# A state-space scan and a long convolution on one core: every fourth time is scanned, three states per block of four are rebuilt, and the whole order is written anew

## Chip, cores and metric

The kernel runs on 1 core of a Trainium2 chip. The metric is device time in microseconds, the median of a few executions. Before the change it is 246.62 us (3 runs, 243.36 to 247.5). A difference is told as a share of the time before.

## What is computed

Two independent halves share one output of 2048 times by 1280 columns, in bfloat16. In the left half a diagonal complex recurrence with 640 states reads x (2048 x 640):

```
Lam_bar = exp(dt * Lam);  Bu = x @ B_bar.T          (complex, 640 states)
h_t = Lam_bar * h_(t-1) + Bu_t                      (t = 0 .. 2047)
y_t = 2 * Re(C h_t) + x_t * Dskip
```

The right half takes q, k, v (2048 x 640 each): k is shifted and weighted with four taps per column, multiplied by v, convolved per column with a kernel of length 2048 (ssm_k, plus a skip ssm_D), and multiplied by q.

## The kernel before

Everything stands in one program of some 500 named steps (`make_plan`), each with an engine and a function. A string, `ORDER`, lists the steps in the order in which they are issued; a step `name@slot` takes that PSUM slot. There are four PSUM tiles of two banks. Each engine runs its own steps in that order and waits on the others by semaphores, so a step that waits holds up all that stands behind it on its engine or DMA queue.

Left half. The 640 states are five blocks j of 128, on the partitions; time lies along the free dimension. x is loaded transposed on SyncE's queue (`load_x`, L372). Time is cut in two chunks c of 1024 and each chunk into odd and even times, so there are four loads of 512 x 640: x01, x00 for the first chunk, x11, x10 for the second. B is loaded (B0 on SyncE, the rest, B1, on ScalarE's queue), transposed by matmuls against an identity (bt) and evicted (bte). For each block n = 5c + j:
- zo: ten matmuls with the odd x (five per real and imaginary part), evicted by ScalarE (zoe) into zo with one column of history.
- z: ten matmuls with the even x and four with diagonal matrices of Lam_bar (diagL, L404 to L408) that fold in the odd input just before, evicted to z (ze).
- rs (`dve_scan`, L424): VectorE turns z by a table of cosines and sines (L419 to L422), which makes the recurrence real, and scans real and imaginary part with the decay rr2 (L430).
- rout (`dve_out`, L433): VectorE turns back; the result is the state at even times.
- od (`dve_odd`, L439): VectorE makes the state at odd times from it, in five instructions (L443 to L447).

The second chunk starts from a carry (L449). Then p (`pe_proj`, L455) multiplies 128 times of either parity by C, with x times a diagonal of Dskip added; ScalarE evicts to one of two yo tiles (L477) and GpSimd stores it (yd, L481).

Right half, for five blocks G of 128 columns: k and v come transposed (kT, vT, SyncE); kS, a copy of k with its halves of partitions swapped (GpSimd's queue); four taps as matmuls with diagonal weights (dS, tap); VectorE multiplies by v from PSUM (kv, L532); the product goes to memory (kvo, L535) and comes back as rows (kvs, L505). The convolution is a Fourier transform in two matmul stages for kv (s1k, s2k) and for the kernel's rows (hs, s1h, s2h), each evicted by ScalarE; VectorE multiplies the spectra (y, L566 to L574, two halves); two inverse stages follow, with a DMA transpose between them (inv, zs, zt, fin); VectorE multiplies by q from PSUM (ob, L608; q's load is qi, L598), in the tile from which GpSimd stores the result (od_, L613).

A DMA is issued by its engine in order, too: SyncE's queue carries all transposing loads and hs, GpSimd's carries kS, kvo, kvs, qi, od_ and yd.

Of the kernel before, what the change touches and what calls it, by code (L numbers as in the profile page):

```python
# [9 lines left out]
ALU = mybir.AluOpType  # L10
# [32 lines left out]
class Kernel:  # L43


    def __init__(self, ctx, tc, out, ins):
# [19 lines left out]
        for n in ("lre", "lim", "dtf", "theta", "rho", "rr", "rr2", "fr", "kf", "sin1", "aph1", "cos1", "nr", "ni", "den",  # L66
                  "t0", "rden", "ra"):
            t(n, [128, NT], f32)
        t("dt_b", [128, NT])
        t("Fi", [128, NT], i32)  # L70
        t("cmul", [128, NT], i32)
        t("phc", [128, NT], i32)
        t("gam", [128, 3, NT], f32)
        t("lam", [128, 3, NT], f32)
        t("lamb", [128, 3, NT])
        t("rots", [128, NT, 2], f32)
        t("rotc", [128, NT, 2], f32)
# [12 lines left out]
        t("dcol_b", [128, 32 * NG])  # L90
# [36 lines left out]
        self.aph = self.zz[:, 7168:8192].bitcast(f32)  # L127
        self.gph = flat(self.Hf).bitcast(i32).rearrange("p (q a b) -> p q a b", q=4, a=4)
# [21 lines left out]
    def load_B(self, eng, lo, hi):  # L150
        for r, ap in enumerate((self.A_B_re, self.A_B_im)):
            eng.dma_start(out=self.Bn[:, r, lo:hi, :], in_=ap.rearrange("(j i) d -> i j d", i=128)[:, lo:hi, :])

    def load_sk(self):
        src = self.B_shift_k.rearrange("(g h d) s -> h d g s", h=2, d=64)
        for v in range(2):
            for h in range(2):
                self.nc.gpsimd.dma_start(out=self.sk_b[64 * h:64 * h + 64, :, v, :], in_=src[h ^ v])

    def pool_consts(self):  # L160
# [3 lines left out]
        g.iota(self.lo, pattern=[[2, CW]], base=0, channel_multiplier=0)  # L164
        g.iota(self.c30[:], pattern=[[0, 1]], base=2 ** 30, channel_multiplier=0)

    def pool_consts2(self):
        g = self.nc.gpsimd
        g.iota(self.c26[:], pattern=[[0, 1]], base=2 ** 26, channel_multiplier=0)
        g.iota(self.cmul[:], pattern=[[0, NT]], base=2 * CW, channel_multiplier=0)  # L170
        g.iota(self.ccol[:], pattern=[[1, 4]], base=0, channel_multiplier=0)
        g.iota(self.r_ph[:].rearrange("p (k r) -> p k r", r=2), pattern=[[4, 16], [0, 2]], base=1, channel_multiplier=0)
        g.iota(self.r_q16[:].rearrange("p (k r) -> p k r", r=2), pattern=[[0, 16], [16, 2]], base=0, channel_multiplier=0)
# [98 lines left out]
    def dve_gamma(self):  # L272
# [3 lines left out]
        ni = self.lam[:, 1, :]  # L276
        v.tensor_scalar_add(out=nr, in0=self.lam[:, 0, :], scalar1=-1.0)
# [29 lines left out]

    def pool_rot(self):
        self.nc.gpsimd.tensor_tensor(out=self.phc[:], in0=self.cmul[:], in1=self.Fi[:], op=ALU.mult)

    def act_rot(self):
        a = self.nc.scalar.activation
        a(out=self.rots[:, :, 0], in_=self.phc[:], func=ACT.Sin, scale=-SC)
        a(out=self.rots[:, :, 1], in_=self.phc[:], func=ACT.Sin, scale=SC)
        a(out=self.ra[:], in_=self.phc[:], func=ACT.Abs, scale=SC)
        for r in range(2):
            a(out=self.rotc[:, :, r], in_=self.ra[:], func=ACT.Sin, bias=self.hpi[:, 0:1], scale=-1.0)
# [54 lines left out]
    def load_x(self, c, p):  # L372
        self.nc.sync.dma_start_transpose(
            out=self.__dict__[f"xT{c}{p}"][:],
            in_=self.x2[2 * CW * c:2 * CW * c + 2 * CW, :].rearrange("(m p) (k d) -> p m k d", p=2, d=128)[p])

    def pe_z(self, n, p, r, ps, last=True):
        c, j = divmod(n, NT)
        xT = self.__dict__[f"xT{c}{p}"]
        for k in range(NT):  # L380
# [506 lines left out]
```

## Time and profile before

| | before |
|---|---|
| median of 3 runs | 246.62 us |
| the profiled execution: its time, its span | 247.58, 245.7 us |
| TensorE busy (pipelined, modelled ends) | 197.2 us, 80% |
| VectorE busy | 180.7 us, 74% |
| ScalarE busy | 152.0 us, 62% |
| GpSimd busy | 64.8 us, 26% |
| DMA, share of 16 engines: SyncE's, GpSimd's, ScalarE's queue | 52.6%, 26.3%, 2.3% |
| granted TensorE clock, mean | 0.961 |

The span is the time from the first to the last instruction of one profiled execution. A busy share is a mean over stages with different limits, so the table alone doesn't tell what the time hangs on: for that one looks at stretches of the span, at what an engine waited for, and at the chain of work that ended last. PE is TensorE, DVE VectorE, ACT ScalarE, POOL GpSimd, SP SyncE; a q behind a name is that engine's DMA queue.

### The profile page before, as it was taken

The numbers are of one execution on the slowest core, as the hardware profiler recorded it, in microseconds if no ns is written. First come the engines' busy times: TensorE is split into PE (matmuls) and PEld (weight loads), VectorE is DVE, ScalarE is ACT, GpSimd is POOL, SyncE is SP. The second block draws the span as 40 slices with busy tenths as digits, with TensorE's granted clock in tenths as the row PEclk, the third lists the DMA queues.
The fourth block names the chain that finished last, engine by engine and source line by source line (L and its number), as shares of the span: only waits on it lengthen the run. The fifth ranks groups of instructions, "written<-read, shape, count | busy, mean of one in ns | idle before, by whom it ended". The sixth has DMA issues, their size and how long they took to land.

```text
span 245.7 us, 5441 instructions
## 1 busy us (share of the span) xinstructions
PE 197.2 (80%) x2295; PEld 140.8 (57%) x2306; DVE 180.7 (74%) x303; ACT 152.0 (62%) x187; POOL 64.8 (26%) x91
## 2 busy tenths in 40 slices
PE   0266996977796699989629999989758999985991
PEld 0162342435444678767426579776756598764770
DVE  2749399999999999999606973897559999950030
ACT  2648395976976657645325888896638999442121
POOL 8897692025000220015051120010501100110231
PEclk9999799999999799999958999999989999999998
DMA  3999999999920689498969989409993503829634
GB/s 57 248 180 24 190 237 224 193 191 228 172 56 2 183 166 111 89 168 240 102 134 196 241 176 221 75 0 124 218 196 72 119 21 65 128 55 185 149 117 121
DMA packets 80698, 34.87 MB, mean 142 GB/s; under 512 B 76001, under 2 KB 77281, under 8 KB 80673
## 3 DMA queue, kind: packets, MB, share of 16 engines
q1 hardware_dynamic: 73936, 18.75, 52.6%
q0 software_dynamic: 4368, 14.46, 26.3%
q10 hardware_dynamic: 2368, 1.31, 2.3%
q8 instruction: 18, 0.29, 0.5%
q14 instruction: 8, 0.06, 0.1%
HBM read 9.52 MB, written 7.86 MB: 71 GB/s over the span
## 4 chain that ended last, share of the span: by engine, by line
DVE 15%; issue 13%; PE 12%; DMA 12%; POOL 2%; ACT 1%; DVEq 1%; POOLq 0%; ACTq 0%
DMA out_dram<-yo 5%; DMA zz<-zz 4%; DMA qb<-in_B_q_dram 3%; PE ps L465 2%; DVE rot L571 2%; DVE Xs L572 2%; PE ps L381 2%; DVE Xs L574 2%; PE ps L527 2%; DVE z L430 2%; DVE vT L532 1%; POOL out_dram L613 1%; DVE rot L419 1%; DVE rot L420 1%; DVE qb L608 1%
## 5 line engine op out<-in xcount | busy, mean ns | idle before, releaser
L381 PE MATMUL ps<-xT,BT 128*128 128x512 bf16 x189 | 48.3, 387 | 6.0 <-ACT zz L144 2.1
L465 PE MATMUL ps<-Cs,h 128*128 128x320 bf16 x320 | 48.3, 299 | 0.0
L381 PEld LDWEIGHTS <-BT 128*128 128x128 bf16 x200 | 19.1, 99 | 28.7 <-issue 5.9
L465 PEld LDWEIGHTS <-h 128*128 128x128 bf16 x320 | 29.3, 98 | 10.2
L477 ACT CAST yo<-ps 128x640 bf16<-128x640 f32 x16 | 11.0, 692 | 38.9 <-PE ps L469 25.7
L608 DVE TENSOR_TENSOR qb<-ps,qb 128x1024 bf16<-128x1024 f32 x10 | 12.1, 1219 | 26.0 <-PE ps L603 16.0
L558 PE MATMUL ps<-As_kv,Gre 128*128 128x128 bf16 x80 | 18.5, 231 | 8.8 <-ACT yo L477 6.6
L564 ACT CAST Xs<-ps 128x1024 bf16<-128x1024 f32 x20 | 19.2, 1028 | 7.2 <-PE ps L561 6.4
L559 PEld LDWEIGHTS <-nGim 128*128 128x128 bf16 x160 | 16.5, 103 | 12.4 <-issue 10.7
L564 ACT CAST Hf<-ps 128x1024 bf16<-128x1024 f32 x20 | 19.5, 1046 | 6.4 <-PE ps L561 5.3
L548 ACT CAST As_h<-ps 128x1024 bf16<-128x1024 f32 x20 | 20.1, 1041 | 5.3 <-PE ps L544 5.3
L590 ACT CAST zz<-ps 128x1024 bf16<-128x1024 f32 x20 | 19.5, 1026 | 3.3 <-PE ps L585 2.5
L548 ACT CAST As_kv<-ps 128x1024 bf16<-128x1024 f32 x20 | 19.5, 1030 | 1.5 <-PE ps L544 1.5
L559 PE MATMUL ps<-As_h,nGim 128*128 128x128 bf16 x80 | 18.3, 229 | 1.3 <-DVE nGim L343 1.3
L532 DVE TENSOR_TENSOR vT<-ps,vT 128x1024 bf16<-128x1024 f32 x10 | 11.9, 1213 | 10.1 <-PE ps L527 10.1
L558 PE MATMUL ps<-As_h,Gre 128*128 128x128 bf16 x80 | 18.3, 229 | 1.3 <-DVE qb L608 1.0
L582 PE MATMUL ps<-Xs,Hre 128*128 128x128 bf16 x80 | 17.6, 219 | 1.4 <-DVE Xs L574 1.4
L561 PE MATMUL ps<-As_kv,Gre 128*128 128x128 bf16 x80 | 18.5, 232 | 0.0
L560 PE MATMUL ps<-As_kv,Gim 128*128 128x128 bf16 x80 | 18.5, 232 | 0.0
L559 PE MATMUL ps<-As_kv,nGim 128*128 128x128 bf16 x80 | 18.5, 232 | 0.0
L560 PE MATMUL ps<-As_h,Gim 128*128 128x128 bf16 x80 | 18.3, 228 | 0.0
L561 PE MATMUL ps<-As_h,Gre 128*128 128x128 bf16 x80 | 18.3, 228 | 0.0
(166 smaller groups left out, 528.8 us busy)
## 6 DMA issues: line engine op xcount, KB each, us to landing
h_st<-in_B_ssm_k_dram SPq DMA_DIRECT2D x10, 256.0 KB, 5.7
qb<-in_B_q_dram POOLq DMA_DIRECT2D x5, 512.0 KB, 6.8
kv_rows<-vT POOLq DMA_DIRECT2D x5, 512.0 KB, 4.7
kv_st<-kv_rows POOLq DMA_DIRECT2D x10, 256.0 KB, 7.1
out_dram<-yo POOLq DMA_DIRECT2D x8, 320.0 KB, 3.4
out_dram<-qb POOLq DMA_DIRECT2D x5, 512.0 KB, 6.8
kS<-kT POOLq DMA_DIRECT2D x10, 129.0 KB, 4.7
zz<-in_A_B_re_dram ACTq DMA_DIRECT2D x1, 640.0 KB, 7.6
```

What stands on the lines that cost most here:

```text
L381: self.nc.tensor.matmul(ps, lhsT=self.BT[:, r, k, j * 128:(j + 1) * 128], rhs=xT[:, k, :], start=(k == 0), stop=(last and k == NT - 1))
L465: mm(o[:, 0:320], lhsT=h[:, p, r, ts], rhs=self.Cs[:, r, j, c0:c0 + 320], start=(j == 0 and r == 0), stop=False)
L532: self.nc.vector.tensor_tensor(out=self.vT[:, ts], in0=ps[:].rearrange("p a n -> p (a n)"), in1=self.vT[:, ts], op=ALU.mult)
L548: self.nc.scalar.copy(out=As[:].rearrange("p k (h s) -> p h k s", h=2)[:, :, :, 16 * q:16 * q + 16], in_=ps[:].rearrange("p h (k s) -> p h ...
L558: mm(o_re, lhsT=self.Gre[:, k1, :], rhs=re, start=True, stop=False)
L559: mm(o_re, lhsT=self.nGim[:, k1, :], rhs=im, start=False, stop=True)
L560: mm(o_im, lhsT=self.Gim[:, k1, :], rhs=re, start=True, stop=False)
L561: mm(o_im, lhsT=self.Gre[:, k1, :], rhs=im, start=False, stop=True)
L564: self.nc.scalar.copy(out=dst[:, :, o:o + 128 * n], in_=ps[:] if n == 4 else ps.rearrange("p (r n) -> p r n", r=2))
L582: mm(o_re, lhsT=self.Hre[:, k1, :], rhs=yre, start=True, stop=False)
L590: self.nc.scalar.copy(out=self.Zs[:, :, 2 * ks[0]:2 * ks[0] + n, :].rearrange("p i k c -> p k i c"), in_=psf.rearrange("p (k i c) -> p k i ...
L608: self.nc.vector.tensor_tensor(out=self.qb[:, :, cs].rearrange("p a (i c) -> p a i c", c=4), in0=ps[:].rearrange("p a n -> p (a n)").rearr ...
```

## The change

- Left half: time is no longer cut into chunks. It is split by its remainder p to 4, so there are four loads of 512 x 640 (x0 to x3, every fourth time), and tiles F{p}{j} hold the input sums and later, in place, the states. Per block j the inputs are summed in the order 1, 2, 3, 0: z1 takes ten matmuls, z2, z3 and z0 take ten and four with diagL that add Lam_bar times the sum before. For z2 of blocks 0 to 2 that addition is made by VectorE instead (zd2, `dve_odd` with q = 1). One scan per block, over 512 columns with the decay rr4, needs z0, and so all four x. The rotation back gives the state at p = 0 in place (h0); three `dve_odd` rebuild the states at p = 1, 2, 3 (h1, h2, h3) with the powers Lam, Lam^2, Lam^3, which a new step `pow` makes. Chunk, carry, history and their steps are gone.
- The projection takes 128 groups of four times; a store holds two of the four remainders.
- B comes block by block: eight loads of 160 KB, all on SyncE's queue, behind x1. lre moves from ScalarE's to GpSimd's queue.
- The shift taps come by one load, and their swapped half by two copies from SBUF to SBUF that wait for it. The skip column ssm_D comes in runs of 61 elements instead of single ones.
- The order of all steps is new.

```
     def load_x(self, p):
         self.nc.sync.dma_start_transpose(out=self.__dict__[f"xT{p}"][:],
                                          in_=self.x2.rearrange("(m p) (k d) -> p m k d", p=NP, d=128)[p])
...
+        prev = None if p == 1 or (p, j) in BYDVE else (self.F(p - 1, j) if p else self.__dict__[f"F3{j}"][:, :, 1:1 + CW])
+        for r in range(2):
+            for k in range(NT):
+                mm(ps[:, r, :], lhsT=self.BT[:, r, k, j * 128:(j + 1) * 128], rhs=xT[:, k, :], start=(k == 0),
+                   stop=(prev is None and k == NT - 1))
+            if prev is not None:
+                mm(ps[:, r, :], lhsT=self.diagL[:, 0, j, :], rhs=prev[:, r, :], start=False, stop=False)
+                mm(ps[:, r, :], lhsT=self.diagL[:, 2 - r, j, :], rhs=prev[:, 1 - r, :], start=False, stop=True)
...
+    def dve_odd(self, p, j, q=0):
+        v = self.nc.vector
+        h, s = self.F(q, j), self.F(p, j)
+        l = [self.lam[:, p - q - 1, i, j:j + 1] for i in range(3)]
+        v.tensor_scalar_mul(out=self.rot_p, in0=h, scalar1=l[0])
+        v.tensor_scalar_mul(out=self.rot_x[:, 0, :], in0=h[:, 1, :], scalar1=l[2])
+        v.tensor_scalar_mul(out=self.rot_x[:, 1, :], in0=h[:, 0, :], scalar1=l[1])
+        v.tensor_tensor(out=s, in0=s, in1=self.rot_p, op=ALU.add)
+        v.tensor_tensor(out=s, in0=s, in1=self.rot_x, op=ALU.add)
...
     def load_sk(self):
-        src = self.B_shift_k.rearrange("(g h d) s -> h d g s", h=2, d=64)
-        for v in range(2):
-            for h in range(2):
-                self.nc.gpsimd.dma_start(out=self.sk_b[64 * h:64 * h + 64, :, v, :], in_=src[h ^ v])
+        g = self.nc.gpsimd
+        g.dma_start(out=self.sk_b[:, :, 0, :], in_=self.B_shift_k.rearrange("(g d) s -> d g s", d=128))
+        for h in range(2):
+            g.dma_start(out=self.sk_b[64 * h:64 * h + 64, :, 1, :], in_=self.sk_b[64 - 64 * h:128 - 64 * h, :, 0, :])
...
+            src = bass.AP(src.tensor, src.offset, [[1, 4], [128, NG], [1, 61]])
+            g.dma_start(out=self.dcol_b[64 * h:64 * h + 64:16, :, 0:61], in_=src)
...
-pc l_lim l_ldt B0 l_lre B1 x01 pc2 dc zer gp1 exp dc2 bt0@0 dt bt1@2 pp rho bte0@0 rr x00 G1 gp0 Fi aRM bte1@2 bt6@0 l_sk bt5@4
+pc l_ldt B0 x1 l_dsk dc l_lre exp l_lim gp2 bt1@0 bt0@2 B1 bte1@0 gp0 bte0@2 B2 B3 gp1 zer z10@2 B4 dt pc2 rho x2 Fi rr G2 tp0
```

On SyncE's queue at the start of the program, behind the first load of B and of x (xT are the loads of x, Cs those of C, h_st the rows of the kernel), there stands before:

```order
L373 DMA_TRANSPOSE xT_142<-in_A_x_dram 128x5x512
L494 DMA_TRANSPOSE kT<-in_B_k_dram 128x2048
L505 DMA h_st<-in_B_ssm_k_dram 64x16x128 x2
L494 DMA_TRANSPOSE vT<-in_B_v_dram 128x2048
L680 DMA_TRANSPOSE Cs<-in_A_C_re_dram 128x5x640
L680 DMA_TRANSPOSE Cs<-in_A_C_im_dram 128x5x640
L373 DMA_TRANSPOSE xT_145<-in_A_x_dram 128x5x512
L373 DMA_TRANSPOSE xT_144<-in_A_x_dram 128x5x512
```

and now, behind x1 and the other eight loads of B:

```order
L361 DMA_TRANSPOSE xT_141<-in_A_x_dram 128x5x512
L445 DMA_TRANSPOSE kT<-in_B_k_dram 128x2048
L445 DMA_TRANSPOSE vT<-in_B_v_dram 128x2048
L629 DMA_TRANSPOSE Cs<-in_A_C_re_dram 128x5x640
L361 DMA_TRANSPOSE xT_147<-in_A_x_dram 128x5x512
L629 DMA_TRANSPOSE Cs<-in_A_C_im_dram 128x5x640
L361 DMA_TRANSPOSE xT_129<-in_A_x_dram 128x5x512
L456 DMA h_st<-in_B_ssm_k_dram 64x16x128 x2
```

The rows h_st have moved behind the last x. The last x (x0, xT_129), which the first scan needs now, has the same transposing loads ahead of it as the last of before (xT_144).

On VectorE, around the first scan of the program (z_154 is block 0's z), there stands before:

```order
L515 TENSOR_TENSOR diagS<-id_70,sk_b 128x512
L291 TENSOR_TENSOR diagD<-ident,dsk_raw 128x640
L419 TENSOR_TENSOR rot<-tabs,z_154 128x1024
L420 TENSOR_TENSOR rot<-tabs,z_154 128x1024
L422 TENSOR_TENSOR rot<-rot 128x512 x2
L430 SCALAR_TENSOR_TENSOR z_154<-rr_84,rot 128x512 x2
```

and now (F_132 is F02, the sum of block 2 at p = 0):

```order
L466 TENSOR_TENSOR diagS<-id_70,sk_b 128x512
L331 TENSOR_SCALAR nGim<-Gim 128x2048
L302 SCALAR_TENSOR_TENSOR Cs<-Cs,gam,As_kv 128x640
L304 SCALAR_TENSOR_TENSOR Cs<-Cs,gam,As_kv 128x640
L382 TENSOR_TENSOR rot<-tabs,F_132 128x1024
L383 TENSOR_TENSOR rot<-tabs,F_132 128x1024
L385 TENSOR_TENSOR rot<-rot 128x512 x2
L392 SCALAR_TENSOR_TENSOR F_132<-rr_84,rot 128x512 x2
```

The diagS here is block 1's; the first block's stands ahead of diagL. The first scan has moved behind both kv products of block 0, three of five blocks of C and nGim.

On GpSimd's queue, in the middle of the program (vT to kv_rows is kvo, kv_rows to kv_st is kvs, out from qb is od_, qb from q is qi, out from yo is yd), there stands before:

```order
L535 DMA kv_rows<-vT 128x2048
L481 DMA out_dram<-yo_148 256x1x640
L613 DMA out_dram<-qb 128x16x128
L501 DMA kS<-kT 64x2x516 x2
L481 DMA out_dram<-yo_147 256x1x640
L598 DMA qb<-in_B_q_dram 128x16x128
L505 DMA kv_st<-kv_rows 64x16x128 x2
L481 DMA out_dram<-yo_147 256x1x640
```

and now:

```order
L452 DMA kS<-kT 64x2x516 x2
L564 DMA out_dram<-qb 128x16x128
L549 DMA qb<-in_B_q_dram 128x16x128
L486 DMA kv_rows<-vT 128x2048
L456 DMA kv_st<-kv_rows 64x16x128 x2
L430 DMA out_dram<-yo_155 128x2x640
L430 DMA out_dram<-yo_154 128x2x640
L564 DMA out_dram<-qb 128x16x128
```

The first two stores of yo have moved behind the last block's store and reload of kv.

## Rows read from the trace of the kernel before

**Rows 1.** Busy time of each engine by stretches: from:to, length, then engines.

```profile
0.00:53.50 53.50, 35.34 (x223) 17.84 (x228) 38.76 (x93) 35.25 (x57) 32.55 (x52) 0.97 1.12 171
53.50:121.10 67.60, 59.35 (x692) 41.92 (x694) 66.51 (x111) 42.75 (x49) 11.53 (x16) 0.97 0.84 143
121.10:180.60 59.50, 49.15 (x717) 38.21 (x720) 36.07 (x49) 41.25 (x45) 12.20 (x15) 0.94 0.82 150
180.60:216.30 35.70, 31.90 (x437) 26.33 (x435) 34.65 (x50) 26.62 (x29) 2.99 (x3) 0.95 0.51 98
216.30:245.70 29.40, 21.45 (x235) 16.54 (x234) 4.70 (x4) 6.08 (x8) 5.49 (x6) 0.96 0.57 124
```

**Rows 2.** VectorE in order of time: start, us; in brackets idle before and releaser.

```profile
116.05 0.69 DVE L419 TENSOR_TENSOR rot<-tabs,z 128x1024 bf16<-128x1024 bf16 x1
...
118.17 0.49 DVE L443 TENSOR_SCALAR rot<-h,lam 128x1024 bf16<-128x1024 bf16 x1
...
120.43 0.68 DVE L515 TENSOR_TENSOR diagS<-id,sk_b 128x512 bf16<-128x512 bf16 x1
131.21 1.23 DVE L532 TENSOR_TENSOR vT<-ps,vT 128x1024 bf16<-128x1024 f32 x1 [10.10 <-PE ps L527]
...
154.63 1.23 DVE L608 TENSOR_TENSOR qb<-ps,qb 128x1024 bf16<-128x1024 f32 x1 [4.80 <-ACT Hf L564]
155.77 1.22 DVE L571 TENSOR_TENSOR rot<-Xs,Hf 128x2048 bf16<-128x2048 bf16 x1
...
159.68 1.23 DVE L571 TENSOR_TENSOR rot<-Xs,Hf 128x2048 bf16<-128x2048 bf16 x1
...
180.62 1.23 DVE L608 TENSOR_TENSOR qb<-ps,qb 128x1024 bf16<-128x1024 f32 x1 [5.23 <-DMA qb<-in_B_q_dram]
181.76 0.68 DVE L419 TENSOR_TENSOR rot<-tabs,z 128x1024 bf16<-128x1024 bf16 x1
...
186.12 1.20 DVE L608 TENSOR_TENSOR qb<-ps,qb 128x1024 bf16<-128x1024 f32 x1
```

**Rows 3.** The chain that ended last, in order of time: start, us, what.

```profile
114.77 11.97 DMA out_dram<-yo
...
164.92 1.16 POOL out_dram L613
...
172.79 7.70 DMA qb<-in_B_q_dram
```

**Rows 4.** SyncE's queue in order of time, the last two loads of x.

```profile
38.31 6.39 SPq L373 DMA_TRANSPOSE xT<-in_A_x_dram  x2
```

**Rows 5.** The tile xT, all four loads.

```profile
DMA to landing us min/median/max: 5.4/9.9/14.5
```

**Rows 6.** DMA issues: out<-in, queue, operation, count, KB each, median us to landing.

```profile
kv_st<-kv_rows POOLq DMA_DIRECT2D x10, 256.0 KB, 7.1
...
zz<-in_A_B_im_dram ACTq DMA_DIRECT2D x1, 640.0 KB, 11.4
...
zz<-in_A_B_im_dram SPq DMA_DIRECT2D x1, 160.0 KB, 5.7
...
sk_b<-in_B_shift_k_dram POOLq DMA_DIRECT2D x4, 2.5 KB, 7.2
```

**Rows 7.** TensorE in order of time, matmuls of z, in the start.

```profile
32.58 4.48 PE L381 MATMUL ps<-xT,BT 128*128 128x512 bf16 x19
```

**Rows 8.** VectorE by line: shapes, count | busy us, mean ns | idle us before.

```profile
L303 DVE SCALAR_TENSOR_TENSOR Cs<-Cs,gam,As_kv 128x640 bf16<-128x640 bf16 x3 | 2.6, 879 | 0.0
...
L343 DVE TENSOR_SCALAR nGim<-Gim 128x2048 bf16<-128x2048 bf16 x1 | 0.7, 686 | 0.0
...
L284 DVE TENSOR_TENSOR gam<-nr,lre 128x5 f32<-128x5 f32 x1 | 0.2, 157 | 0.0
```

**Rows 9.** The tile vT: its transposing loads and its stores to kv_rows.

```profile
DMA to landing us min/median/max: 3.2/6.1/13.8
```

**Rows 10.** The chain that ended last, its last product of spectra.

```profile
215.60 0.70 DVE Xs L574
```

More of the change, by code (lines that the diff above doesn't have):

```diff
@@ L22 @@
 CW = 512
-NCH = 2
+NP = 4
+BYDVE = {(2, j) for j in range(3)}
 NG = 5
 PAD = 16
-NZ = 3
-NH = 6
 NPS = 4
-SPLIT = set()
 class Plan:
@@ L306, in dve_cs @@
                                op0=ALU.mult, op1=ALU.add)
[L308 to L317, printed above, removed]
     def pool_tab(self, j):
@@ L369, in ev_bt @@
             self.copy(eng, self.BT[:, :, ks[0], 128 * js[0]:128 * js[-1] + 128], ps[:, :, 0:128 * n])
[L372 to L380, printed above, removed]
-            self.nc.tensor.matmul(ps, lhsT=self.BT[:, r, k, j * 128:(j + 1) * 128], rhs=xT[:, k, :],
-                                  start=(k == 0), stop=(last and k == NT - 1))
@@ new lines, in make_plan @@
+    for j in range(NT):
+        for i, q in enumerate(xo):
+            byd = (q, j) in BYDVE
+            last = f"{'zd' if (xo[i - 1], j) in BYDVE else 'ze'}{xo[i - 1]}{j}" if i else ""
+            A(f"z{q}{j}", "PE", (14 if i and not byd else 10) * P512, [f"x{q}"] + ([last, "dL"] if i and not byd else []) + bt_of[j],
+              lambda ps, q=q, j=j: K.pe_z(q, j, ps), take=f"z{q}{j}", group=f"Z{q}{j}")
+            A(f"ze{q}{j}", "ACT", EV, [f"z{q}{j}", "zer"], lambda ps, q=q, j=j: K.nc.scalar.copy(out=K.F(q, j), in_=ps[:]), give=f"z{q}{j}",
+              group=f"Z{q}{j}")
+            if byd:
+                A(f"zd{q}{j}", "DVE", 2.26, [f"ze{q}{j}", last, "lam"], lambda q=q, j=j: K.dve_odd(q, j, q - 1), group=f"Z{q}{j}")
+        A(f"rs{j}", "DVE", 3 * TT + 0.1 + 2 * SCAN, [f"ze0{j}", f"tab{j}", "pow"], lambda j=j: K.dve_scan(j), group=f"A{j}")
+        A(f"h0{j}", "DVE", 3 * TT + 0.18, [f"rs{j}"], lambda j=j: K.dve_out(j), group=f"A{j}")
+        for q in range(1, NP):
+            A(f"h{q}{j}", "DVE", 2.26, [f"h0{j}", f"{'zd' if (q, j) in BYDVE else 'ze'}{q}{j}", f"{'zd' if ((q + 1) % NP, j) in BYDVE else 'z'}{(q + 1) % NP}{j}"], lambda q=q, j=j: K.dve_odd(q, j), group=f"A{q}{j}")
@@ new lines, in make_plan @@
+    ys = [(i, x) for x in range(2) for i in range(4)]
+    for y, (i, x) in enumerate(ys):
+        for q in (2 * x, 2 * x + 1):
+            A(f"p{i}{q}", "PE", 20 * P320 + 0.3, [f"h{q}{j}" for j in range(NT)] + cs_all + ["dD"],
+              lambda ps, i=i, q=q: K.pe_proj(i, q, ps), take=f"p{i}{q}", group=f"P{x}")
+            A(f"yo{i}{q}", "ACT", 0.6, [f"p{i}{q}", f"yd{ys[y - 2][0]}{ys[y - 2][1]}" if y > 1 else ""],
+              lambda ps, y=y, q=q: K.act_yo(y % 2, q, ps), give=f"p{i}{q}", group=f"P{x}")
+        dma(f"yd{i}{x}", "POOL", 0.68, 0.9, [f"yo{i}{q}" for q in (2 * x, 2 * x + 1)], lambda y=y, i=i, x=x: K.store_yo(y % 2, i, x), group=f"P{x}")
```

339 lines of the change are left out of this document (128 added, 211 removed).

## Prediction

> **What bounds the kernel now.** I read the table of stretches first, then VectorE's rows in order of time around its longest waits, then the chain of waits for what ended those, then SyncE's queue and the landing times of the loads. In the table of stretches [rows 1] the reader is to see that VectorE is the one engine that is full while the others are not: 66.51 of 67.6 us between 53.5 and 121.1, and 34.65 of 35.7 between 180.6 and 216.3. Between them, from 121.1 to 180.6, it works 36.07 of 59.5 us. So the kernel has four stretches: a start up to 53.5 that is bound by loads (DMA share 1.12, TensorE 35.34 and VectorE 38.76 of 53.5), two that are bound by VectorE, a middle one with holes, and a tail of 29.4 us after VectorE's last product of spectra, which ends at 216.3 [rows 10]; in the tail VectorE works 4.7 us.
>
> The holes stand in VectorE's own rows [rows 2]: 10.10 us before 131.21, 4.80 before 154.63 and 5.23 before 180.62. In the chain of waits [rows 3] the first is a store: the output tile yo issued at 114.77 takes 11.97 us to land, ScalarE may not fill that tile again before, the PSUM banks stay full, and TensorE stands. The last is a pair of transfers in a row: the store of block 1's result is issued at 164.92, the load of the next block's q into the same tile only at 172.79, and takes 7.70. VectorE's idle time between 53.5 and 216.3 is 162.8 - (66.51 + 36.07 + 34.65) = 25.6 us: these three (20.1) and 5.5 in small pieces.
>
> **What the change does to VectorE's work.** The starts of neighbouring rows give what an operation takes from VectorE [rows 2]: a rotation back 118.17 - 116.05 = 2.12; a rebuilt state 120.43 - 118.17 = 2.26; a rotation and scan 186.12 - 181.76 = 4.36; a product of spectra 159.68 - 155.77 = 3.91; a PSUM product (ob, kv) 155.77 - 154.63 = 1.14. Before, ten blocks each take one scan, one rotation back and one rebuilt state: 10 x 8.74 = 87.4. After, five blocks take a scan and a rotation back each, 15 states are rebuilt, and three more such five-instruction groups (zd2) fold time 1 into time 2 on VectorE instead of TensorE: 5 x 6.48 + 18 x 2.26 = 73.1. Gone as well are the carry, its copies and the history copies (14 tiny instructions, some 2 us); new is the power table, 16 instructions on 128x5, at the 0.16 us of a like one [rows 8] 2.6. Net about 14 us off VectorE.
>
> That the rebuilt states are added in place (an operand is also the result) is shown by no row; the nearest is the rebuilt state of before with its own result tile, so its 2.26 is taken. Reading and writing one tile could cost something: bounds 2.2 and 2.5 for each of 18, 1 us down, 4 up.
>
> **When the first scan starts.** Before, VectorE has done 38.76 us by 53.5, among it two scans, two rotations back and one rebuilt state (15.2). After, these have to wait, since a scan now needs all four loads of x. What stands ahead of the first scan instead is three zd2 groups (6.8), the power table (2.6), the copy for nGim (0.7 [rows 8]) and three of the five blocks of C (six instructions at 0.88 [rows 8], 5.3): 15.4. So the same 39 us of work is done before the first scan, and with the same 14.7 us of waiting it would start at 53.5. A new wait stands in that queue: diagS needs the shift taps, which now come in two hops, the second issued by GpSimd only after the first has landed; one such load took 7.2 us [rows 6]. Behind diagS on VectorE stand diagL, gamma, the powers and everything up to the scan; behind the second hop on GpSimd stand the phases and kS, which needs kT anyway. A second hop costs 0 to 7.2; I take 2.5, a third, as the 14.7 us of waiting cover part of it. First scan: 56.0.
>
> Do the loads allow that? The four x loads before were issued by 38.31 + 6.39 = 44.7 [rows 4] and the last landed 5.4 us after its own issue [rows 5], near 47. After, x0 has the same transfers ahead of it but for the first h rows, which stand behind it now. The start is full of transfers (DMA share 1.12), so the order moves, not the sum: x0 near 46. Fourteen matmuls at 4.48 / 19 = 0.236 [rows 7] and an eviction of 1 us make 50.5, so this is hidden by VectorE's own 56.0 with 5.5 us to spare. The eight matmuls more (248 against 240) cost TensorE 1.9 us, beside its idle time.
>
> B comes in eight loads of 160 KB on SyncE behind x1, not two of 640 KB on ScalarE's queue. The last of the small pair before landed 5.7 us after its issue, the last of the large pair 11.4 [rows 6], both while x shared the engines. I take the sum as unchanged, 0, with 0 and 6 as bounds. The Trainium skill, "DMA: Bandwidth & Descriptors", section Bandwidth, says loads should be batched to a mebibyte and gives 138 GB/s at 64 KB against 341 at 1 MB; by it the 1.31 MB of the eight would take up to 9.5 instead of 3.8 us, an estimate from that page. If that went through to the scan whole, the time would be 5.7 us above mine, 238, inside the forecast's own range below; I give it a tenth of that case. The rows of before cannot tell it apart, because no small load ran there alone.
>
> **From the first scan to the last product of spectra.** VectorE's work: 5 scans 21.8, 5 rotations back 10.6, 15 rebuilt states 33.9, 10 products 39.1, 14 PSUM products 16.0, two blocks of C 3.5, the small ones (nHim, three diagS, had) 3.2: 128.1. Before, 137.2 were left at 53.5. So the start gives most of the saving back, and what remains is 9 us; the rest must come from the holes, of which each has a successor:
> - The store of yo. GpSimd's order puts the first two stores behind the reload for block 4, so they go out about 0.6 + 5 + 1.7 + 0.7 = 8 us after the last kv product, and land by 20 if they take the 11.97 of [rows 3]. TensorE reaches the block that needs the tile after 14 groups of 0.9 and one projection, 15 us later. VectorE has y3 and three rebuilt states for that stretch, so 5 us of wait on ScalarE reach it in part: 0 to 5, taken 2 in place of 10.1.
> - The wait for q. From the store of a result to the next q landed it was 180.5 - 164.9 = 15.6 [rows 3]. Between ob0 and ob1 VectorE has two products, two kv and a rebuilt state, 12.4: a hole of 3.2 in place of 5.2.
> - A new one: TensorE's first kv transform stands ahead of the taps of block 1, and its rows come by a store and a reload of 7.1 [rows 6]. With the kv product 6 us ahead of the scan, the landing comes 9.6 after it begins; VectorE wants the taps after a scan, two blocks of C and a rotation back, 10.0, and the taps take 1.3 more. 0 to 4, taken 2.
> - The 4.8 and the 5.5 of small pieces stay.
> Idle: 2 + 3.2 + 2 + 4.8 + 5.5 = 17.5, against 25.6.
>
> **The tail.** After the last product there stand four inverse groups, six projections, two fin groups and two stores on either side: 29.4 again.
>
> **Sum.** 56.0 + 128.1 + 17.5 + 29.4 = 231.0 of span, and 1.9 around it as before (247.58 against 245.7): 232.9, 14.7 us under the profiled execution. The median of the runs is 246.62, 0.96 below that execution, so 232.
>
> **Rivals.**
> - The holes move but stay as long. VectorE, TensorE and ScalarE carry nearly equal loads between the scans and the first projection, where a late one makes the other two late. Against it stands that the three long holes have named causes and the order puts work in them. With the whole second hop and idle 25.6: 60.7 + 128.1 + 25.6 + 29.4 + 1.9 = 245.7, on the median 244.7.
> - Late landings pass through, slower than before. Its place is the reload of each block's kv rows and the transpose of v ahead of it: the tile v moved in 3.2 to 13.8 us [rows 9], and each block chains v, store, reload, transform. A tighter order leaves less cover. With the spread of some 7 us a block over a middle landing of 6.1, and 2.6 hidden, five blocks lose 22: 255. It decides from 4.2 us a block, above which the kernel is over 2% slower; 3 us a block makes it equal. For it: the DMA share, 0.84 and 0.82 in the middle, rises when the same bytes move in less time. Against: at 0.84 VectorE was still 98% busy up to 121.1.
> - Better packed: the second hop hidden and idle 8, with only the small pieces and the wait for q left: 53.5 + 126 + 8 + 29.4 + 1.9 = 218.8, so 218.
>
> **How the numbers follow.** Forecast 0.52 (226 to 239 by the bounds above), long holes 0.22, late landings 0.12, better packed 0.14. A difference under 2%, 4.9 us, can't be told from none here. Faster by over 2% (below 241.7): 0.52 + 0.14 and a quarter of the second case, 0.71; within 2%: 0.17; slower: 0.12. The range for 8 in 10 is 220 to 247: it leaves out the last case and the better half of the third.
>
> **What would show it.** First scan (rotation L382) on VectorE near 56, x0 landed before 50; VectorE's busy time about 166 of the span; no wait over 5 us between scan and last product; the last product near 201; a tail of 29 to 30 us. The forecast is wrong if the first scan starts after 62, if VectorE idles over 25 us behind it, or if the rebuilt states take over 2.5 us each.

## The result, and the profile after

The changed kernel takes 224.81 us (median of four executions, 224.6 to 236.5), the kernel before 246.12 in the same comparison: a ratio of 0.917 with the interval 0.907 to 0.927, faster by about 20.5 us. The forecast was 232.0 with the range 220 to 247. The profiled execution of that comparison was the longest, 236.5 us, so I profiled the unedited kernel again; the rows below are of that execution, 229.47 us with 227.7 of span, which is still above the median (the others beside it took 220.48 to 230.15). Executions more than 1.5% above the fastest of their kernel are left out of every ratio.

> The changed kernel once more, unedited, for a profile of an undisturbed execution. Theory (the forecast's own sum): the start takes what it was said to take, first scan at 56 to 58 us, and VectorE then stays under 12 us idle up to the last product of spectra (the forecast's 17.5 was too much); time 224 to 226 us. Rival: the saving stands in the start instead, first scan before 52 us, and the idle time behind it is the forecast's 17 to 18 us; the same time.

Measured: 227.39 us (220.48 to 230.15); over the eight executions of both comparisons the median is 225.2. The scan came where the theory had it, the idle time did not. The table of stretches of the changed kernel, cut at the first scan on VectorE and at the end of the last product of spectra (as in [rows 1]: behind the length stand the busy time and, in brackets, the instructions of TensorE, its weight loads, VectorE, ScalarE and GpSimd, then the granted clock, the DMA share and GB/s):

```profile
0.00:57.40 57.40, 41.84 (x242) 20.50 (x243) 37.07 (x102) 36.50 (x56) 31.68 (x51) 0.97 0.90 159
57.40:198.60 141.20, 133.97 (x1847) 102.00 (x1846) 125.96 (x192) 107.27 (x118) 26.66 (x32) 0.96 0.86 154
198.60:227.70 29.10, 21.63 (x231) 16.65 (x228) 4.72 (x5) 7.03 (x9) 5.65 (x6) 0.98 0.62 136
sum 227.70, PE 197.44 PEld 139.14 DVE 167.75 ACT 150.79 POOL 63.99; mean PE 65.81 PEld 46.38 DVE 55.92 ACT 50.26 POOL 21.33
```

The first scan starts at 57.4, VectorE then works 125.96 of 141.2 us, the tail is 29.1. The reader is to look at TensorE's column too: 133.97 of the 141.2 us. Before, from 53.5 to 216.3, TensorE stood 22.4 of 162.8 us [rows 1]; now it stands 7.2 of 141.2. Over the whole span it does the same work (197.19 before, 197.44 now), so its idle time falls from 48.5 to 30.3 us, by 18.2 where the spans differ by 18.0. For an engine whose work stays the same that is arithmetic (GpSimd's, 64.77 and 63.99 us, does the same) and names no cause. VectorE's work fell by 12.9, from 180.69 to 167.75.

The same stretch in the execution of 236.5 us is 7.8 us longer with nearly the same work, so VectorE idles 22.5 us of it instead of 15.2:

```profile
57.30:206.30 149.00, 135.06 (x1847) 102.52 (x1846) 126.48 (x193) 107.32 (x118) 26.25 (x32) 0.95 0.88 146
```

VectorE's longer waits in the execution of 229.47 us, in order of time; they answer to [rows 2]:

```profile
93.35 1.23 DVE L483 TENSOR_TENSOR vT<-ps,vT 128x1024 bf16<-128x1024 f32 x1 [3.90 <-PE ps L478]
...
136.73 1.23 DVE L559 TENSOR_TENSOR qb<-ps,qb 128x1024 bf16<-128x1024 f32 x1 [3.68 <-ACT As_kv L499]
...
156.02 2.36 DVE L559 TENSOR_TENSOR qb<-ps,qb 128x1024 bf16<-128x1024 f32 x2 [1.12 <-PE ps L512]
...
199.16 2.36 DVE L559 TENSOR_TENSOR qb<-ps,qb 128x1024 bf16<-128x1024 f32 x2 [0.55 <-DMA qb<-in_B_q_dram]
216.68 2.36 DVE L559 TENSOR_TENSOR qb<-ps,qb 128x1024 bf16<-128x1024 f32 x2 [15.17 <-DMA qb<-in_B_q_dram]
```

None of the three long holes of before is left here; in the execution of 236.5 us, though, VectorE waits 5.92 us for a q:

```profile
184.35 1.23 DVE L559 TENSOR_TENSOR qb<-ps,qb 128x1024 bf16<-128x1024 f32 x1 [5.92 <-DMA qb<-in_B_q_dram]
```

In the execution of 229.47 us the longest wait between the scan and the last product is 3.90 us, and it stands at a place that the forecast didn't name; three views explain it: TensorE's waits by what ended them (sum, times, longest), GpSimd's issue of the reload (two loads) with TensorE's rows behind it, and the stretches of 2 us around them.

```profile
PE ps L373 <- DVE lre L215: 6.7, 1, 6.7
PE ps L495 <- DMA kv_st<-kv_rows: 5.4, 3, 3.0
```

```profile
76.29 2.14 POOL L456 DMA_DIRECT2D kv_st<-kv_rows  x2
...
87.25 0.38 PE L478 MATMUL ps<-kS,diagS 64*64 64x512 bf16 x1
...
90.79 0.61 PE L495 MATMUL ps<-R,kv_st 64*128 64x128 bf16 x7 [3.00 <-DMA kv_st<-kv_rows]
91.32 0.63 PE L478 MATMUL ps<-kT,diagS 64*64 64x512 bf16 x1
```

```profile
88.00:90.00 2.00, 0.00 (x0) 0.00 (x0) 1.45 (x2) 0.00 (x0) 0.00 (x0) 1.00 1.21 65
90.00:92.00 2.00, 1.21 (x15) 0.72 (x19) 0.00 (x0) 0.52 (x1) 0.00 (x0) 0.50 1.39 163
92.00:94.00 2.00, 2.00 (x23) 0.81 (x16) 0.65 (x1) 0.62 (x2) 0.00 (x0) 0.50 0.12 17
94.00:96.00 2.00, 2.00 (x22) 2.00 (x20) 1.97 (x4) 1.25 (x2) 0.57 (x1) 0.50 0.67 141
96.00:98.00 2.00, 2.00 (x32) 2.00 (x30) 2.00 (x4) 1.48 (x2) 0.00 (x0) 0.79 1.18 373
```

The reload of block 1's kv rows, issued from 76.29 on, lands only at 90.8. TensorE stands 3.0 us for it, and then works at a granted clock of 0.50, the lower of its two levels (1.2 GHz), until about 96.7: a row of 64x512 operands takes 0.63 us in place of 0.38. By the clock column some 3 of those 6 us are lost as well, so this late landing cost TensorE about twice its wait. In the execution of a_q2 below the same reload was issued from 76.08 on and TensorE did not wait for it. Whether such landings are what sets executions of this kernel 10 us apart is not shown: those near 220 us left no trace.

### The profile page after: what moved, and what is told of

Same layout as the page of the kernel before. It is cut to its first block, busy times and chain, and to the rows that moved or that the text cites. A ratio compares the mean times of both kernels' runs of the same rounds, so it can differ in the third digit from the quotient of the medians.

```text
span 234.7 us, 5462 instructions
## 1 busy us (share of the span) xinstructions
PE 198.7 (85%) x2314; PEld 139.0 (59%) x2314; DVE 168.8 (72%) x296; ACT 150.6 (64%) x182; POOL 63.7 (27%) x89
## 3 DMA queue, kind: packets, MB, share of 16 engines
q1 hardware_dynamic: 75088, 20.06, 56.4%
## 4 chain that ended last, share of the span: by engine, by line
PE 37%; DMA 34%; DVE 12%; issue 9%; POOL 4%; ACT 2%; POOLq 0%; DVEq 0%; ACTq 0%
DMA kv_st<-kv_rows 10%; DMA zz<-zz 7%; PE ps L373 7%; PE ps L417 6%; PE ps L478 4%; DMA lim_raw<-in_A_Lambda_im_dram 4%; DMA qb<-in_B_q_dram 3%; DMA out_dram<-qb 3%; PE ps L495 3%; DMA sk_b<-sk_b 3%; DVE qb L559 3%; PE ps L509 2%; DMA kT<-in_B_k_dram 2%; PE ps L512 2%; PE ps L510 2%
## 5 line engine op out<-in xcount | busy, mean ns | idle before, releaser
L373 PE MATMUL ps<-xT,BT 128*128 128x512 bf16 x200 | 50.5, 396 | 6.3 <-DVE lre L215 6.3
L417 PE MATMUL ps<-Cs,F 128*128 128x320 bf16 x320 | 49.9, 306 | 1.6 <-DVE qb L559 1.6
L417 PEld LDWEIGHTS <-F 128*128 128x128 bf16 x320 | 30.0, 100 | 12.5 <-issue 1.7
L648 ACT CAST F<-ps 128x1024 bf16<-128x1024 f32 x20 | 19.9, 1011 | 7.6 <-PE ps L377 5.4
L486 POOL DMA_DIRECT2D kv_rows<-vT x5 | 2.9, 577 | 58.2 <-DVE vT L483 58.2
L533 PE MATMUL ps<-Xs,Hre 128*128 128x128 bf16 x80 | 18.1, 226 | 0.0
L534 PE MATMUL ps<-Xs,nHim 128*128 128x128 bf16 x80 | 18.1, 226 | 0.0
L535 PE MATMUL ps<-Xs,Him 128*128 128x128 bf16 x80 | 18.0, 225 | 0.0
L536 PE MATMUL ps<-Xs,Hre 128*128 128x128 bf16 x80 | 18.0, 225 | 0.0
L509 PE MATMUL ps<-As_h,Gre 128*128 128x128 bf16 x80 | 17.6, 220 | 0.2 <-DVE qb L559 0.2
L509 PE MATMUL ps<-As_kv,Gre 128*128 128x128 bf16 x80 | 17.5, 219 | 0.1
L512 PE MATMUL ps<-As_h,Gre 128*128 128x128 bf16 x80 | 17.6, 219 | 0.0
```

Of the source, the lines that this page charges most:

```text
L373: mm(ps[:, r, :], lhsT=self.BT[:, r, k, j * 128:(j + 1) * 128], rhs=xT[:, k, :], start=(k == 0), stop=(prev is None and k == NT - 1))
L417: mm(ps[:, b, 0:320], lhsT=self.F(p, j)[:, r, ts], rhs=self.Cs[:, r, j, c0:c0 + 320], start=(j == 0 and r == 0), stop=False)
L509: mm(o_re, lhsT=self.Gre[:, k1, :], rhs=re, start=True, stop=False)
L512: mm(o_im, lhsT=self.Gre[:, k1, :], rhs=im, start=False, stop=True)
L533: mm(o_re, lhsT=self.Hre[:, k1, :], rhs=yre, start=True, stop=False)
L534: mm(o_re, lhsT=self.nHim[:, k1, :], rhs=yim, start=False, stop=True)
```

## The experiments

**q no longer waits for the store of the result.** Odd blocks load q into the transposed B, which is dead by then, and the loads stand earlier in the order (qi1 behind kS4, qi2 behind yd00, qi3 behind yd30, qi4 behind yd11).

```
+        self.qb1 = self.BT[:].rearrange("p r k n -> p (r k n)")[:, 0:2048].rearrange("p (a c) -> p a c", a=16)
-        self.nc.gpsimd.dma_start(out=self.qb[:], in_=self.q2[...
+        self.nc.gpsimd.dma_start(out=self.qt(G), in_=self.q2[...
+    def qt(self, G):
+        return self.qb1 if G % 2 else self.qb[:]
```

> The next block's q is loaded into a second tile (the transposed B, dead by then) for odd blocks, and its load is issued one block earlier, so it no longer waits for the store of the result. Theory (store of block 3's result and then the load of q are what the last product of the tail waits for): the tail behind the last product of spectra shrinks by 4 to 8 us, time 217 to 221 us. Rival (the transposes of the last block's rows end as late, or other loads give way to the earlier q): tail shorter by less than 2 us, time 223 to 226 us.

Measured: 220.46 us (219.75 to 222.09), ratio to before 0.896 (0.891 to 0.902). Its table of stretches and its last waits:

```profile
57.00:191.60 134.60, 131.12 (x1849) 100.04 (x1847) 126.69 (x193) 107.22 (x119) 26.94 (x33) 0.99 0.85 162
191.60:218.00 26.40, 21.40 (x231) 16.57 (x228) 4.73 (x5) 6.93 (x9) 5.31 (x6) 1.00 0.66 150
```

```profile
203.54 1.22 DVE L563 TENSOR_TENSOR qb<-ps,qb 128x1024 bf16<-128x1024 f32 x1 [9.66 <-PE ps L555]
207.11 1.23 DVE L563 TENSOR_TENSOR qb<-ps,qb 128x1024 bf16<-128x1024 f32 x1 [2.34 <-PE ps L555]
```

The tail fell from 29.1 to 26.4 us, so less than the 4 to 8 expected: once q is there, ob4 waits for TensorE, which is full until 213. The larger part of what lies between the two profiled executions, 6.6 of 9.7 us, stands ahead of the tail (134.6 against 141.2), and it is not shown to come from this edit: in a_sk1 (the next experiment), where q waits as in the changed kernel, the stretch is as short, and VectorE idles 9.7 us of it.

```profile
54.20:189.70 135.50, 131.20 (x1847) 100.05 (x1846) 125.81 (x192) 107.19 (x118) 25.87 (x32) 0.99 0.84 161
```

The median is near the theory's upper end; seven of the unedited kernel's eight executions lie above all four of a_q2's, the eighth, 220.48 us, among them. The four lie within 2.4 us of each other, where the unedited kernel's lay within 9.7 in the same comparison, but three runs built on a_q2 spread by 7.4 to 14.7 us (q2_dcol1, q2_sk1, q2_lessP), so a narrower spread is not shown. TensorE's waits for bank space held by ob fell from 3.4 to 0.4 us.

**The taps in one hop**, on the changed kernel and on a_q2.

```
-        g = self.nc.gpsimd
-        g.dma_start(out=self.sk_b[:, :, 0, :], in_=self.B_shift_k.rearrange("(g d) s -> d g s", d=128))
-        for h in range(2):
-            g.dma_start(out=self.sk_b[64 * h:64 * h + 64, :, 1, :], in_=self.sk_b[64 - 64 * h:128 - 64 * h, :, 0, :])
+        src = self.B_shift_k.rearrange("(g h d) s -> h d g s", h=2, d=64)
+        for v in range(2):
+            for h in range(2):
+                self.nc.gpsimd.dma_start(out=self.sk_b[64 * h:64 * h + 64, :, v, :], in_=src[h ^ v])
```

> The shift taps are loaded in one hop, by four loads from DRAM as in the kernel before, all else as in the changed kernel. Theory (the second hop is what diagS waits for, 2.5 us on the forecast's path): diagS and all behind it on VectorE start 2 to 3.4 us earlier, first scan 2 to 3 us earlier, time 222 to 223 us. Rival (x0, the kv rows or the tables are as late as the scan, so the wait only moves): first scan within 1 us of the changed kernel's, time 224 to 226 us.

> a_q2 with the shift taps in one hop. Theory (the second hop holds diagS and, through VectorE's order, the first scan; the run a_sk1 had the scan 3 us earlier): 2 to 3.5 us under a_q2, 217 to 218.5 us. Rival (TensorE's work from the first x on is the bound and the earlier scan only makes VectorE wait later): within 1 us of a_q2, 219.5 to 221.5 us.

Measured: a_sk1 225.7 us (221.45 to 231.91), ratio 0.901 (0.894 to 0.908); q2_sk1 219.51 (214.73 to 222.91), ratio 0.880 (0.871 to 0.889). The first scan did start earlier, at 54.2 and 54.4; the unedited kernel waits for the second hop in the first of these rows, and a_sk1 starts its first scan in the second:

```profile
29.91 0.83 DVE L466 TENSOR_TENSOR diagS<-id,sk_b 128x512 bf16<-128x512 bf16 x1 [3.16 <-DMA sk_b<-sk_b]
```

```profile
54.19 0.69 DVE L382 TENSOR_TENSOR rot<-tabs,F 128x1024 bf16<-128x1024 bf16 x1
```

So the hop costs the first scan 3 us. Whether it costs the kernel as much is not settled: both ratios fell by 1.6 points against their partners (some 4 us), but each rests on two of four executions, the medians over all four hardly moved, and the unedited kernel's fastest execution in a_sk1's comparison (220.48) lies below both of those two.

**The load of the imaginary eigenvalues first**, on q2_sk1: in the order, l_lim stands ahead of exp.

> q2_sk1, and the load of the imaginary eigenvalues is issued first on ScalarE's queue, ahead of the exponential that waits for log dt, so that VectorE's conversion does not stand for it until 12 us. The candidate that is to beat both kernels. Theory (VectorE's order and TensorE's first evictions stand behind that conversion): 2 to 4 us under a_q2, 216.5 to 218.5 us. Rival (the first x lands at 12 us in any case, so the wait only changes its name): as q2_sk1, 217 to 220 us.

Measured: 216.83 us, ratio 0.881 (0.875 to 0.887), first scan at 52.9; five of six executions took 215.33 to 219.19 and one 399.43. This is 29 us under the kernel before and some 8 under the changed kernel: the lowest median found. It is within the theory's range, and just under the rival's, and the ratio is nearly q2_sk1's 0.880, so the share of this load beside q2_sk1 stays unclear.

**VectorE's folding ahead of the scan left to TensorE** (diagL and the eigenvalues moved ahead of z20, z11 ahead of z21).

```
-BYDVE = {(2, j) for j in range(3)}
+BYDVE = set()
```

> The three groups on VectorE that fold time 1 into time 2 ahead of the first scan go; TensorE adds those products with its diagonal, as it does for the other blocks (12 matmuls more, diagL built earlier). VectorE loses 6.8 us of work ahead of the first scan. Theory (the forecast's: VectorE's own work sets the first scan, loads and TensorE are covered): first scan 4 to 7 us earlier, time 218 to 221 us. Rival (the start is bound by landings, VectorE's work there lies in their shadow): first scan less than 2 us earlier, or the gain is given back as idle time behind it; time 223 to 227 us.

Measured: 224.29 us (221.3 to 226.35), ratio 0.902 (0.895 to 0.909), profiled at 225.6. VectorE's work ahead of the scan fell to 26.21 us, and the scan came at 53.9, 3.5 us earlier: of the 10.9 us of work that went, most came back ahead of the scan, where VectorE idles 6.06 us for the taps and 6.16 for the first kv product. Behind it the 3.5 us were not given back in this execution; the stretch to the last product is 140.4 us, where it was 141.2:

```profile
53.90:194.30 140.40, 133.01 (x1851) 100.70 (x1849) 125.91 (x191) 108.24 (x119) 24.87 (x30) 0.99 0.87 153
```

The median lies in the rival's range. It is 0.5 us under that of the first comparison and 3.1 under the unedited kernel's in its own (227.39), and the ratio is 1.5 points lower, again on two of four executions. So it is open whether the rival holds: the gain lies between nothing and some 3.5 us.

**Less work on VectorE, on TensorE, on both**, built on a_q2. Each leaves out a part of the arithmetic, so its output is another; only the time is of use.

```
         v.tensor_tensor(out=s, in0=s, in1=self.rot_p, op=ALU.add)
-        v.tensor_tensor(out=s, in0=s, in1=self.rot_x, op=ALU.add)
+        if q:
+            v.tensor_tensor(out=s, in0=s, in1=self.rot_x, op=ALU.add)
```

```
+            h = As is self.As_h
...
-            mm(o_re, lhsT=self.nGim[:, k1, :], rhs=im, start=False, stop=True)
+            if not h:
+                mm(o_re, lhsT=self.nGim[:, k1, :], rhs=im, start=False, stop=True)
...
```

> Built on a_q2 (220.46 us). Each of the 15 rebuilt states leaves out its last addition (the cross terms of the complex product), 0.61 us of VectorE each, 9.2 us in all, behind the first scan; TensorE does the same matmuls. Theory (TensorE is what is full between the first scan and the last product, 131 of 134.6 us, and VectorE's holes are only its remainder): less than 2.5 us faster, 218 to 221 us, VectorE's idle time grows by 7 to 9 us. Rival (VectorE bounds this stretch, as the forecast summed it): 7 to 9 us faster, 211 to 213.5 us.

> Built on a_q2 (220.46 us). The transform of the filter h leaves out its two products with the imaginary part, 160 matmuls of 128 columns, some 0.055 us each when they follow one another, 8.8 us of TensorE over all five blocks; VectorE does the same work. Theory (TensorE bounds from the first scan to the end): 5 to 8.8 us faster, 211.5 to 215.5 us; less than the whole because VectorE has only some 8 us of slack there. Rival (VectorE bounds): less than 2 us faster, 218.5 to 221 us.

> Both cuts at once on a_q2: the last addition of each rebuilt state (9.2 us of VectorE) and the two imaginary products of h's transform (8.8 us of TensorE) are left out. Each alone gave 1 to 2.5 us. Theory (TensorE and VectorE carry nearly the same load behind the first scan, each hides what is taken from the other): 6 to 10 us under a_q2, 210 to 214 us. Rival (neither bounds; the chain of each block, v's transpose, store of kv, reload, transform, sets the pace): within 4 us of a_q2, 216.5 to 221 us.

Measured: q2_lessD 219.87 us (218.39 to 222.03), ratio 0.893 (0.886 to 0.901); q2_lessP 219.69 (217.31 to 232.05), ratio 0.886 (0.880 to 0.892); q2_lessDP 222.1 (215.21, 217.81, 226.38 and 482.39), ratio 0.883 (0.873 to 0.892), each against a_q2's 0.896. The stretch of q2_lessD behind the first scan, and TensorE's longest waits in the whole execution:

```profile
56.20:190.20 134.00, 130.37 (x1842) 99.76 (x1846) 118.38 (x178) 106.72 (x118) 26.86 (x33) 0.99 0.84 163
```

```profile
PE ps L374 <- DVE lre L216: 6.6, 1, 6.6
PE ps L342 <- DMA zz<-in_A_B_re_dram: 4.4, 1, 4.4
PE ps L480 <- ACT F L653: 2.6, 1, 2.6
PE ps L497 <- DMA kv_st<-kv_rows: 1.9, 1, 1.9
```

VectorE works 118.38 us there, 8.3 less than in a_q2, and the stretch is 134.0 us long, where it was 134.6: nearly all of the removed work came back as idle time. TensorE is busy 130.37 us of it, and no wait of its is longer than 2.6 us but for the two in the start. VectorE does not bound a_q2 behind the scan. But taking 8.8 us from TensorE gave only some 2.5 (1.0 point of the ratio, less than its theory's 5 to 8.8), and taking both gave some 3.4 (1.4 points), each on two of four executions, so the theory of two equal engines falls too; the rival's range fits the ratio. The profiles of these two runs are of their longest executions (232.05 and 482.39 us), so no row shows what took the place of the work removed. One explanation left is the chain of transfers of each block, of which the wait at 87.8 above is one case; another is ScalarE's evictions, 106.72 of the 134.0 us, which TensorE's banks wait for. No run here changes either alone, so neither is shown.

**The hole of the kernel before, closed by itself.** In the kernel before, p0_2_1_0, p0_2_0_0, their evictions and the store yd0_2 move to just before p0_3_1_0, and p0_2_0_0 takes PSUM slot 4, where it had 6.

> The kernel before; the one pair of projections that waited for the landing of the store of yo, with its evictions and its store, is moved behind the next blocks' work in the order, nothing else. It tells what the 10.1 us hole of the kernel before was worth by itself. Theory (the forecast's: a hole closed is time gained, VectorE bounds there): 6 to 10 us faster than the kernel before, 236 to 240 us. Rival (the work behind it is short of TensorE or of other landings, so the wait only moves): less than 3 us faster, 243 to 247 us.

Measured: 249.87 us (248.04 to 252.12), ratio 1.018 (1.007 to 1.028): slower by 0.7 to 2.8%, a miss for theory and rival alike. Waits of its VectorE and its table of the middle:

```profile
124.87 1.23 DVE L532 TENSOR_TENSOR vT<-ps,vT 128x1024 bf16<-128x1024 f32 x1 [4.57 <-PE ps L527]
...
149.40 1.22 DVE L608 TENSOR_TENSOR qb<-ps,qb 128x1024 bf16<-128x1024 f32 x1 [4.23 <-ACT Hf L564]
...
164.53 1.23 DVE L608 TENSOR_TENSOR qb<-ps,qb 128x1024 bf16<-128x1024 f32 x1 [6.27 <-PE ps L603]
```

```profile
121.10:180.60 59.50, 54.73 (x738) 41.81 (x738) 36.38 (x48) 39.65 (x45) 11.97 (x15) 0.94 0.75 139
```

The hole shrank from 10.10 to 4.57 us and the product behind it came 6.3 us earlier, at 124.87. By 164.53 VectorE waits 6.27 us for TensorE, and the last product ends at 217.1, where it ended at 216.3. In the same 59.5 us, from 121.1 to 180.6 as in [rows 1], VectorE did as much work as there (36.38 against 36.07) while TensorE was busy 54.73 in place of 49.15. TensorE had the deferred work still to do. Nor did its own stand go. The kernel before has one of 6.58 us, which ends at the first of these rows; the edited kernel has three in its place, 6.0 us together, for ScalarE's evictions and for kS:

```profile
127.57 0.27 PE L558 MATMUL ps<-As_kv,Gre 128*128 128x128 bf16 x1 [6.58 <-ACT yo L477]
```

```profile
115.78 0.62 PE L544 MATMUL ps<-R,kv_st 64*128 64x128 bf16 x16 [2.75 <-ACT As_kv L548]
118.19 0.27 PE L558 MATMUL ps<-As_kv,Gre 128*128 128x128 bf16 x1 [1.79 <-ACT As_kv L548]
...
122.91 0.58 PE L527 MATMUL ps<-kS,diagS 64*64 64x512 bf16 x1 [1.46 <-DMA kS<-kT]
```

So the edit took the store out of the hole, but not the hole out of TensorE's time; what it would be worth with TensorE kept busy, this run does not tell. The two profiled executions differ by 0.5 us of span (246.2 against 245.7); why the median became slower rather than equal, I did not find.

**Two parts of the change undone, on a_q2**: B's later blocks in two loads of 640 KB, and the skip column loaded element by element.

```
+        lo, hi = ((0, 1), (1, NT))[j] if j < 2 else (0, 0)
...
-            eng.dma_start(out=self.Bn[:, r, j, :], in_=ap[128 * j:128 * j + 128, :])
+                eng.dma_start(out=self.Bn[:, r, lo:hi, :], in_=ap.rearrange("(j i) d -> i j d", i=128)[:, lo:hi, :])
```

> Built on a_q2: B's four later blocks in two loads of 640 KB at the first block's place in SyncE's queue, not in eight of 160 KB; one part of the change undone. Theory (the forecast's 0: the same bytes, the engines share them): within 1.5 us of a_q2, 219 to 222 us, first z of block 1 to 4 not earlier. Rival (the rule that large loads are better): 2 to 6 us faster, 214.5 to 218.5 us. A third way (the blocks arrive together and late, so TensorE's first z waits): 2 to 5 us slower.

> Built on a_q2: the skip column is loaded element by element as in the kernel before; one part of the change undone. Theory (the forecast gave this part nothing, its transfer lies behind other loads and is wanted only at block 0's h): within 1.5 us of a_q2, 219 to 222 us. Rival (its many small packets hold up the transposes at 20 to 40 us, where the DMA share is over 1): 2 to 5 us slower, 222.5 to 225.5 us.

Measured: q2_B2 218.57 us (217.27 to 220.55), ratio 0.890 (0.881 to 0.898), first scan at 56.4; q2_dcol1 221.75 (219.78 to 227.15), ratio 0.897 (0.889 to 0.904), first scan at 55.6. Both intervals hold a_q2's 0.896. The column is worth nothing that these runs can tell, as forecast. The large loads of B moved the scan by 0.6 us and the median by 1.9, between the two expectations, and by the lower end of the interval (0.881) a gain of up to some 4 us is open. The Trainium skill, "DMA: Bandwidth & Descriptors", section Bandwidth, says to batch loads to a mebibyte; the 5.7 us that the forecast estimated from it are not there.

## Why the prediction was right, and where it was not

The direction and the range held; the time was 7.2 us too long. Term by term, against the profiled 227.7:
- First scan 56.0, measured 57.4. VectorE's work ahead of it is 37.07 (39 forecast) and the waiting 20.3, not 14.7 and 2.5; the longest wait there, 5.07 us, is for the imaginary eigenvalues (L214 below). The second hop was taken at 2.5; its wait is 3.16 and undoing it gave 3.2. Some 5 us of the work are small operations held up beside GpSimd's (last section), which no term named; but the 38.76 us of before, from which the forecast counted, held about as much. The other two rows below are of the kernel before, where the first rotation and scan stand beside GpSimd's tables (28.1 to 38.1 us); the next took 0.76 and 2.33, 3.2 us less, and two more rows there (22.11 and 31.41) are 0.84 and 0.85 longer than their like.

```profile
12.34 0.17 DVE L214 CAST lim<-lim_raw 128x5 f32<-128x5 bf16 x1 [5.07 <-DMA lim_raw<-in_A_Lambda_im_dram]
```

```profile
32.97 2.33 DVE L422 TENSOR_TENSOR rot<-rot 128x512 bf16<-128x512 bf16 x2
35.22 3.97 DVE L430 TENSOR_TENSOR_SCAN z<-rr,rot 128x512 bf16<-128x512 f32 x2
```

- VectorE's work behind the scan 128.1, measured 125.96; over the span 166 forecast, 167.75 measured. Rebuilding a state in place costs no more than before: the five instructions of one, up to the next row, take 45.07 - 42.82 = 2.25, forecast 2.26.

```profile
42.82 0.48 DVE L403 TENSOR_SCALAR rot<-F,lam 128x1024 bf16<-128x1024 bf16 x1
...
45.07 0.82 DVE L290 TENSOR_TENSOR diagD<-ident,dsk_raw 128x640 bf16<-128x640 bf16 x1
```

- Idle time behind the scan 17.5, measured 15.2, but with other members, and not the same in each execution: 22.5 in that of 236.5 us, 9.7 in a_sk1's of 222.22. The successor of the store of yo and the first kv transform, 2 us each, did not come. The waits for q are 1.12 and 0.55, not 3.2 (the first stands under TensorE's name, but that q was issued at 149.81 and landed 6.1 us later); in the execution of 236.5 us one is 5.92, over the 5 us that the forecast allowed. The 3.90 for block 1's late reload was in no term, nor was that behind the 3.68 at 136.73, ahead of which TensorE waits 0.88 and 1.49 us for block 3's.
- Tail 29.4, measured 29.1, with a wait in it that the forecast did not name: the store of block 3's result and the load of block 4's q behind it (15.17 us of wait).
- These terms are 3.4 us of the error (232.9 against 229.47). The other 3.7 come from the last step, "0.96 below that execution": it put the changed kernel's median as near to a profiled execution as before's, and it lies 4.7 us below this one.

The step that failed in its reason is the first, carried over to the changed kernel: that VectorE's rows set the time between the scans and the last product, with holes to be added to its work. The sum came out since VectorE's work and idle time make up the stretch whoever bounds it, and the guess for the idle time was near. That was luck: in three profiled executions the idle time runs from 9.7 to 22.5 us. And 8.3 us less work on VectorE changed nothing (q2_lessD), while the 10.1 us hole of before, shortened to 4.57, gave nothing (b_p2late). In the kernel before no run lightened VectorE, so whether it bounded the stretch up to 121.1 there stays open. Which part of the change brought the 20.5 us, the lighter VectorE or the new order, no run separates.

Two readings of the forecast need a word. It calls VectorE the one full engine of two stretches, but [rows 1] has TensorE busy 59.35 of 67.6 and 31.90 of 35.7 us in them. And by its own numbers late landings cost over 2% from 3.9 us a block on, not 4.2 (251.5 less 232, by five); nothing else rests on that.

Of the rivals, better packed (218) is as near to the median as the forecast, 6.8 and 7.2 us away: its idle time of 8 is near a_sk1's 9.7, but its second hop was not hidden. The long holes did not come in this execution. Late landings pass through, as the second rival said, at the reload of the kv rows; but three times in this execution, for 5.4 us of TensorE's waits and the lower clock behind the longest, not 22 us.

## What to carry to other kernels

An engine that is nearly full need not be the bound: VectorE works 126.69 of 134.6 us in a_q2, and 8.3 us less work gave nothing. Take work off each full engine in turn, and time that, before naming one. A hole with a named cause is worth its length only if no other engine still has the same work to do behind it; move the one step that makes the hole and time it before counting it as a gain. A tile that is stored and loaded again in turn puts two transfers in a row into each block's chain. And one profiled execution can lie several us from the next of the same kernel: hold a term against more than one trace before calling it right.

## What the runs showed of the hardware

VectorE's smallest operations were held by GpSimd's. The rows of VectorE and then of GpSimd in the unedited kernel:

```profile
35.72 0.17 DVE L286 TENSOR_TENSOR gam<-gam,rden 128x5 f32<-128x5 f32 x1
35.80 1.73 DVE L283 TENSOR_TENSOR gam<-lam,lre 128x5 f32<-128x5 f32 x1
...
37.65 1.00 DVE L285 TENSOR_TENSOR gam<-gam,t 128x5 f32<-128x5 f32 x1
38.68 0.96 DVE L286 TENSOR_TENSOR gam<-gam,rden 128x5 f32<-128x5 f32 x1
```

```profile
36.45 1.05 POOL L310 TENSOR_TENSOR kv_st<-Xs,Fi 128x512 int32<-128x512 int32 x1
37.58 1.04 POOL L311 TENSOR_TENSOR kv_st<-kv_st,c 128x512 int32<-128x512 int32 x1
38.58 1.04 POOL L310 TENSOR_TENSOR qb<-Xs,Fi 128x512 int32<-128x512 int32 x1
```

An operation on 128x5 takes 0.17 us alone and 0.96 to 1.73 beside GpSimd's tables, and each ends just when GpSimd's ends (38.65 and 38.62). The Trainium skill, "SBUF — State Buffer", section "Who interferes with whom", says that a VectorE instruction with two SBUF inputs contends with a GpSimd instruction that reads SBUF, over a shared pair of ports that is locked for one of them at a time; the trace agrees.

The granted clock does not tell all: in the execution of 482.39 us it is 1.00 throughout, while the 512-column matmuls of z took a mean of 835 ns, against 394 in the unedited kernel; the longest single one there took 634. What slowed them no row shows.
